# The last inverse stage of a long convolution: 64 outputs per weight, high and low constants side by side

## The chip, the core and the metric

The kernel runs on one core of a Trainium2 chip. Its time is the device time of one execution in microseconds (us), the median of the runs shown. The engines of the core have short names here, as in the profile: PE is TensorE (matmuls; PEld is its loading of weights), ACT is ScalarE, DVE is VectorE, POOL is GpSimd, SP is SyncE. SP does no arithmetic; it issues transfers (DMA). ACT and POOL can issue transfers too, each on a queue of its own. Matmuls write to PSUM, which has eight banks; everything else lives in SBUF, 128 partitions (rows) wide, or in DRAM.

## The reference

Four layers are applied to `x` of 2048 positions by 576 channels. Layers 1 and 3 add a Fourier mixing of the normalised input, layers 2 and 4 add a gated long convolution:

```python
def _A_ref(x, dft_seq_re, dft_seq_im, dft_hid_re, dft_hid_im):
    a = jnp.einsum("bsd,ed->bse", x, dft_hid_re)
    b = jnp.einsum("bsd,ed->bse", x, dft_hid_im)
    return jnp.einsum("ts,bse->bte", dft_seq_re, a) - jnp.einsum("ts,bse->bte", dft_seq_im, b)

def _B_ref(q, k, v, shift_k, ssm_k, ssm_D):
    ...                                    # k_shift: causal convolution of k with 4 taps
    kv = k_shift * v
    y = irfft(rfft(kv, 2 * S) * rfft(ssm_k.T, 2 * S))[:S]    # per channel
    return q * (y + kv * ssm_D)

x = x + _A_ref(_layernorm(x), ...)
x = x + _B_ref(_layernorm(x), B_k, B_v, B_shift_k, B_ssm_k, B_ssm_D)
x = x + _A_ref(_layernorm(x), ...)
x = x + _B_ref(_layernorm(x), B_k, B_v, B_shift_k, B_ssm_k, B_ssm_D)
```

(The transform is written in one line here; the reference uses real FFTs over a padded axis.) What multiplies `q`, the row `y + kv * ssm_D`, does not depend on `x`. Both gated layers use the same one, so the kernel computes it once.

## The kernel before

All data are fp32. A matmul takes its operands rounded to a shorter format (fp32r), so the kernel splits a number into a high part (an ACT copy that rounds) and a low part (a DVE subtraction), and forms high x high, high x low and low x high. The helper `split` does this (L98, L99); `act_split` does it in the stages described here (its lines in the profile are L512 and L518).

**The main line of work** is the first mixing layer (`layer`, L300). A step n of its loop loads one 128x512 block of the sequence matrix (`load_c`, on SP's queue), splits it (L98, L99), and multiplies four column blocks of the input (accumulated in the banks `s0` to `s3`) and a remainder (bank `rm`) with it. A block border comes every 16 steps: the `s` banks are evacuated by ACT and DVE. What results is multiplied by the hidden matrix in halves of 288 columns (`hidden`, L276), 27 matmuls into one bank `bk`, which DVE adds to the residual row (L287).

**The side line** is the long convolution (`branch`, a generator). Whoever runs the main line takes a piece of it whenever its planned share is due: the numbers that the generator yields are planned costs, `I2_COST` = 2.0 for a piece of the last stage. They set the order in which work is laid out, not a time. The convolution is a transform of 4096 points in two steps each way:

- a first stage (`f1_products`) that stores its result `td` in DRAM;
- 64 rounds of a middle stage, 32 for each half of the channels. A round loads a row group of `td` ("feed"), splits it, transforms the kernel's part (`mid_kernel`) and the signal's part (`mid_signal`), multiplies them as complex numbers on DVE (L531 to L534), rounds the product (`mid_round`), transforms it back (`mid_inverse`) and stores it in DRAM as `vd` (L549, ACT's queue). Each transform is three matmuls of 128x288 into one bank `bk`;
- the last inverse stage, 32 products (`i2_products`, L551), one for each half of the channels and each of 16 residues j. A product loads a feed from `vd`, splits it, multiplies it by constants, copies the bank to a tile `vo` and stores that as a piece of the row `yb[j]`.

In the last stage a feed holds two halves c (288 columns each) for 128 frequency rows. The output of a product is 128 positions, so the constants of c are a 128x128 weight `fc[:, c]` (high) and another `fc[:, 2 + c]` (low):

```python
for c in range(2):
    mm(ps[:, :HD], fc[:, c, :], vf[0][:, cs], c == 0, False)
    mm(ps[:, :HD], fc[:, c, :], vf[1][:, cs], False, False)
    mm(ps[:, :HD], fc[:, 2 + c, :], vf[0][:, cs], False, c == 1)
```

**Order and resources.** `feeds` is the list of rounds and products in order: from the 37th round on, every second round is followed by a product of the first half of the channels, ten in all, and the other 22 products stand behind the last round. Constants come on POOL's queue (`load_fr`), feeds on SP's (`load_after`, which places a load behind the latest load of the sequence matrix). The banks `bk` are three and are given out in turn to the hidden halves, the transforms of the middle stage and the products. The ring `vo` has three tiles, shared by `mid_inverse` and the products; a tile is free again when its store has landed. ACT's work on this line is kept in written order (`act`, L509). After the last round, the rings of feeds and constants grow to four tiles each.

Rows of `yb` are read back later, when the gated layers are formed (`gated`, L656).

Of the kernel before, what the change touches and what calls it, by code (L numbers as in the profile page):

```python
# [10 lines left out]
F32 = mybir.dt.float32  # L11
# [4 lines left out]
P = 128  # L16
HP = P // 2
S = 2048
# [47 lines left out]
def fnet_h3_kernel(ctx: ExitStack, tc: tile.TileContext, x, c_mat, w_re, w_im, k_pad, v, shift_k,  # L66
# [16 lines left out]
    def bank():  # L83
        return psp.tile([P, NT], F32, tag="b", bufs=3, name="bk")
# [114 lines left out]
        return t  # L199

    t_d = dr.tile([P, 2 * J, 2 * D], F32, name="td")
    v_d = [dr.tile([P, J, 2, HD], F32, name=f"vd{h}") for h in range(2)]
    yb_d = [dr.tile([P, D], F32, name=f"yb{j}") for j in range(J)]
    xa_d = [dr.tile([P, D], F32, name=f"xa{j}") for j in range(J)]
    xb_d = [dr.tile([P, D], F32, name=f"xb{j}") for j in range(J)]
# [143 lines left out]
    def branch():  # L349
# [142 lines left out]
        at = lay(m1, at, ("yf", D, 2))  # L492
        fc_at = at
        at = lay(flts, SC_AT + CRAW * NT, ("res", D, 2))
        lay(flts, at, ("land", D, 2), ("kk", D, 2), ("vo", HD, 3), ("p2", HD, 1))
        mc = quads(ring["mc"]())
        load_fr(mc, midc)
        lo, hi = slice(0, 64), slice(64, 128)
# [21 lines left out]
        def mid_kernel(df):  # L520
            pk, kk = mid_half(df, HD), two(ring["kk"]())
            act(kk[:, 0, :], pk[:, :HD], AF.Copy)
            act(kk[lo, 1, :], kk[hi, 0, :], AF.Copy)
            act(kk[hi, 1, :], kk[hi, 0, :], AF.Copy, scale=-1.0)
            act(kk[hi, 0, :], kk[lo, 0, :], AF.Copy)
            return kk

        def mid_signal(df, kk):
            px = mid_half(df, 0)
            p1, p2 = kk[:, 0, :], ring["p2"]()  # L530
            nc.vector.tensor_tensor(p1, px[:, :HD], p1, OP.mult)  # L531
            nc.vector.tensor_tensor(p2[lo], px[hi, :HD], kk[hi, 1, :], OP.mult)  # L532
            nc.vector.tensor_tensor(p2[hi], px[lo, :HD], kk[lo, 1, :], OP.mult)  # L533
            nc.vector.tensor_tensor(p1, p1, p2, OP.add)  # L534
            return p1

# [5 lines left out]
        def mid_inverse(hf, qg, yf):  # L542
            pv = bank()
            mm(pv[:, :HD], mc[:, 2, :], yf[:, 0, :], True, False)
            mm(pv[:, :HD], mc[:, 2, :], yf[:, 1, :], False, False)
            mm(pv[:, :HD], mc[:, 3, :], yf[:, 0, :], False, True)
            vo = ring["vo"]()
            act(vo, pv[:, :HD], AF.Copy)
            nc.scalar.dma_start(v_d[hf][4 * qg:4 * qg + 4].rearrange("q j c d -> (q j c) d"), vo)  # L549

        def i2_products(hf, j, fc, vf):  # L551
            yo = ring["vo"]()
            ps = bank()
            for c in range(2):
                cs = slice(c * HD, (c + 1) * HD)
                mm(ps[:, :HD], fc[:, c, :], vf[0][:, cs], c == 0, False)
                mm(ps[:, :HD], fc[:, c, :], vf[1][:, cs], False, False)
                mm(ps[:, :HD], fc[:, 2 + c, :], vf[0][:, cs], False, c == 1)
            act(yo, ps[:, :HD], AF.Copy)
            nc.scalar.dma_start(yb_d[j][:, hf * HD:(hf + 1) * HD], yo)  # L560

        mids = [(0, hf, qg) for hf in range(2) for qg in range(32)]
        late = [(1, 0, j) for j in range(J)]
# [10 lines left out]
        def load_feed(i):  # L574
            if i < len(feeds):
                kind, hf, q = feeds[i]
                landed[i] = ring["land"]()
                load_after(landed[i], v_d[hf][:, q].rearrange("p c d -> p (c d)") if kind else
                           t_d[4 * q:4 * q + 4, :, hf * D:(hf + 1) * D].rearrange("m j d -> (m j) d"))

        def load_fc(k):
            if k < len(rows):
                fcs[k] = quads(ring["fc"]())
                load_fr(fcs[k], i2c[rows[k]])

        def split_feed(i):
# [13 lines left out]
        for i, (kind, hf, q) in enumerate(feeds):  # L600
            df = halves.pop(i)
            if kind:
                i2_products(hf, q, fcs.pop(used), df)
                load_fc(used + ahead)
                used += 1
            else:
                if len(yfs) == MID_LAG:
                    mid_inverse(*yfs.pop(0))
                    yield 0.4
                kk = mid_kernel(df)  # L610
                if product is not None:
                    yfs.append((*product[:2], mid_round(product[2])))
                yield 1.6
                product = hf, q, mid_signal(df, kk)
            split_feed(i + 2)
            if i >= I2_FIRST - 8 and feed_ahead == 3:
                tiles = [ring["land"]() for _ in range(3)]
                if tiles[0] is third:
                    ring["land"], feed_ahead = Ring(tiles[1:]), 2
                    lay(m1, fc_at, ("fc", 4 * P, 2))  # L620
                    load_fc(0)
                    load_fc(1)
            if feed_ahead == 2:
                feed_ahead = 2.5
            else:
                load_feed(i + int(feed_ahead) + 2)
            if i == last_mid:
                yield 0.4
                mid_inverse(*yfs.pop(0))
                yfs.append((*product[:2], mid_round(product[2])))  # L630
                while yfs:
                    yield 0.4
                    mid_inverse(*yfs.pop(0))
                for name, t, at, words in (("fc", m1, spare, 4 * P), ("land", flts, kk_at, D)):
                    old = ring[name]
# [452 lines left out]
def _constants():  # L1088
# [5 lines left out]
    n = (16 * p[None, :, None] + j[:, None, None]) * (4 * q[None, None, :] + 1) % 8192  # L1094
    at = (2 * np.pi * n / 8192).transpose(0, 2, 1)
    at = at[:, np.concatenate([[2 * g, 2 * g + 1, HP + 2 * g, HP + 2 * g + 1] for g in range(HP // 2)])]
# [5 lines left out]
    i1 = np.zeros((2, 2, 2 * J, 2, 2, J, 2))  # L1102
# [6 lines left out]
    th = 2 * np.pi * (j[:, None] * j[None, :] % J) / J  # L1109
    c, s = np.cos(th), np.sin(th)  # L1110
    for a in range(2):
        for b in range(2):
            i1[0, a, b::2, b, a, :, 0] = c
            i1[1, a, b::2, b, a, :, 0] = -s
            i1[0, a, b::2, b, a, :, 1] = s
            i1[1, a, b::2, b, a, :, 1] = c
    m = [*_parts(f2.reshape(P, P)), *_parts(i1.reshape(P, P))]
    return f1c, i2c, np.stack(m, axis=1)

# [39 lines left out]
```

## Time and profile before

| | |
|---|---|
| median of three runs | 1194.99 us (1194.62 to 1196.27) |
| the profiled execution | 1195.03 us, span of its instructions 1193.3 us |
| PE busy | 1172.4 us, 98% of the span |
| DVE busy | 840.3 us, 70% |
| ACT busy | 661.1 us, 55% |
| moved by DMA | 259.85 MB, 218 GB/s over the span |

The page counts an engine as busy while an instruction of it is in flight. Matmuls overlap, so the busy share of PE does not say how fast it works; the chain of waits gives what each matmul costs when they follow one another. In the profile, an instruction is named by its line and by its tiles, output first: `bk<-mid` are the matmuls of the middle and of the last stage (their operands lie in the region `mid`), `bk<-w,u` those of the hidden halves, `s<-mats` and `rm<-mats` those of the main line. `flts` is the region in which `vo`, the feeds and the raw blocks of the sequence matrix lie. L75 is the helper of all matmuls, L168 that of most loads on SP.

### The profile page before, as it was taken

How to read it: one execution, taken by the hardware profiler on the slowest of the kernel's cores; microseconds unless marked ns; L12 is line 12 of the kernel's file. 1: busy time of each engine (PE TensorE's matmuls, PEld its weight loads, DVE VectorE, ACT ScalarE, POOL GpSimd, SP SyncE). 2: the span in 40 equal slices, each digit the busy share in tenths (PEclk: the TensorE clock that was granted, in tenths of full speed). 3: DMA queues.
4: the chain of work that ended last, by engine and by line, in shares of the span. 5: the costliest groups of instructions: out<-in, count | busy, mean ns of one | idle time of the engine just before them, and what ended most of it. 6: DMA issues, size and time to landing. Idle time of an engine off the chain costs nothing.

```text
span 1193.3 us, 18055 instructions
## 1 busy us (share of the span) xinstructions
PE 1172.4 (98%) x6248; PEld 996.3 (83%) x6248; DVE 840.3 (70%) x1498; ACT 661.1 (55%) x1311; POOL 75.6 (6%) x116
## 2 busy tenths in 40 slices
PE   7999999999999999999999999999999999999997
PEld 5776667888888888888988898888888888889997
DVE  7899983679777677685347756865776777774764
ACT  7865655679877668775435666634444445450210
POOL 2210000000000000001101121000000000001111
PEclk9999999999999999999999999999999999999999
DMA  9869898546666656648957676872672777895621
GB/s 327 306 199 311 263 295 269 167 133 188 217 194 211 206 174 203 207 133 272 295 193 236 230 246 226 267 260 71 220 277 76 220 278 258 248 334 158 217 86 41
DMA packets 142846, 259.85 MB, mean 218 GB/s; under 512 B 15649, under 2 KB 43553, under 8 KB 142754
## 3 DMA queue, kind: packets, MB, share of 16 engines
q1 hardware_dynamic: 102674, 205.45, 53.1%
q10 hardware_dynamic: 33168, 42.63, 10.3%
q0 software_dynamic: 6912, 10.62, 3.5%
q8 instruction: 49, 0.80, 0.3%
q14 instruction: 43, 0.35, 0.1%
HBM read 191.99 MB, written 66.65 MB: 217 GB/s over the span
## 4 chain that ended last, share of the span: by engine, by line
PE 76%; ACT 3%; DVE 1%; issue 1%; DMA 0%; POOLq 0%; ACTq 0%; DVEq 0%; SPq 0%
PE s L75 43%; PE bk L75 30%; PE rm L75 4%; ACT flts L512 1%; ACT mid L512 1%; ACT u L98 0%; DMA wd<-w 0%; ACT mats L98 0%; DVE mid L518 0%; DVE flts L534 0%; DVE flts L533 0%; DVE flts L531 0%; DVE flts L532 0%; DVE mats L99 0%; POOLq L1155 0%
## 5 line engine op out<-in xcount | busy, mean ns | idle before, releaser
L75 PE MATMUL s<-mats 128*128 128x512 f32 x2088 | 540.9, 395 | 2.4 <-DVE mats L99 0.8
L75 PEld LDWEIGHTS s<-mats 128*128 128x128 f32 x2088 | 380.9, 188 | 84.8 <-issue 10.4
L99 DVE TENSOR_TENSOR mats<-flts,mats 128x512 fp32r<-128x512 f32 x206 | 141.1, 689 | 63.8 <-ACT mats L98 62.5
L98 ACT ACTIVATE mats<-flts 128x512 fp32r<-128x512 f32 x206 | 128.5, 629 | 82.0 <-PE bk L75 35.0
L75 PE MATMUL bk<-mid 128*128 128x288 f32 x768 | 131.9, 298 | 2.4 <-ACT flts L512 1.6
L75 PEld LDWEIGHTS bk<-mid 128*128 128x128 f32 x768 | 116.9, 188 | 20.0 <-ACT flts L512 6.3
L75 PE MATMUL bk<-w,u 128*128 128x288 f32 x864 | 121.0, 296 | 0.4 <-DVE w L241 0.4
L75 PEld LDWEIGHTS bk<-w,u 128*128 128x128 f32 x864 | 117.5, 188 | 4.0 <-ACT flts L512 1.2
L518 DVE TENSOR_TENSOR mid<-flts,mid 128x576 fp32r<-128x576 f32 (+1 forms) x149 | 93.5, 628 | 34.9 <-ACT mid L512 30.9
L512 ACT ACTIVATE flts<-bk 128x288 f32<-128x288 f32 x160 | 62.1, 404 | 86.8 <-PE bk L75 77.7
L75 PE MATMUL rm<-mats 128*128 128x512 f32 x304 | 94.8, 391 | 0.0
L512 ACT ACTIVATE flts<-flts 64x288 f32<-64x288 f32 x192 | 85.0, 443 | 5.5
L512 ACT ACTIVATE mid<-flts 128x576 fp32r<-128x576 f32 (+1 forms) x148 | 80.4, 575 | 7.6 <-DMA flts<-td 3.2
L451 ACT ACTIVATE flts<-bf 128x384 f32<-128x384 f32 (+1 forms) x104 | 43.2, 463 | 45.6 <-PE bf L75 45.5
L287 DVE TENSOR_TENSOR flts<-flts,bk 128x288 f32<-128x288 f32 x48 | 21.8, 454 | 65.9 <-PE bk L75 65.8
L75 PE MATMUL bk<-mats 128*128 128x288 f32 (+1 forms) x376 | 67.8, 317 | 0.0
L75 PEld LDWEIGHTS rm<-mats 128*128 128x128 f32 x304 | 56.9, 188 | 12.3 <-DVE flts L273 0.2
L75 PE MATMUL s<-t,mats 128*128 128x512 f32 x264 | 64.9, 389 | 0.0
L184 POOL TENSOR_TENSOR flts<-flts 128x1 f32<-128x1 f32 x35 | 29.2, 834 | 522.0 <-DVE flts L183 520.0
L75 PE MATMUL bk<-mats,t 128*128 128x288 f32 (+1 forms) x368 | 59.3, 303 | 0.0
L75 PEld LDWEIGHTS bk<-mats 128*128 128x128 f32 x376 | 55.5, 188 | 3.4
L75 PEld LDWEIGHTS s<-t,mats 128*128 128x128 f32 x264 | 49.5, 188 | 10.3
(145 smaller groups left out, 1467.5 us busy)
## 6 DMA issues: line engine op xcount, KB each, us to landing
flts<-in_c_mat SPq DMA_DIRECT2D x148, 256.0 KB, 3.6
ph<-in_c_mat SPq DMA_DIRECT2D x54, 512.0 KB, 4.5
flts<-in_c_mat SPq DMA_DIRECT2D x30, 512.0 KB, 5.0
flts<-td SPq DMA_DIRECT2D x53, 288.0 KB, 3.0
td<-flts ACTq DMA_DIRECT2D x36, 384.0 KB, 4.5
vd<-flts ACTq DMA_DIRECT2D x64, 144.0 KB, 2.5
flts<-vd SPq DMA_DIRECT2D x32, 288.0 KB, 4.6
mid<-in_i2c POOLq DMA_DIRECT2D x32, 256.0 KB, 4.9
```

The lines of the kernel that those rows point to most:

```text
L75: return nc.tensor.matmul(ps, lhsT, rhs, start=first, stop=last, skip_group_check=more).ins
L98: a = nc.scalar.activation(h, src, AF.Copy).ins
L99: return a, nc.vector.tensor_tensor(l, src, h.bitcast(F32), OP.subtract).ins
L184: pows.append(nc.gpsimd.tensor_tensor(rs, ve, mhalf, OP.pow).ins)
L287: added[:] = [nc.vector.tensor_tensor(r[:, cs], r[:, cs], ps[:, :HD], OP.add).ins]
L451: stored[:] = [nc.scalar.activation(so[:, i, :], ps[i], AF.Copy).ins]
L512: last_act.append(nc.scalar.activation(*args, **kw).ins)
L518: nc.vector.tensor_tensor(l, src, h.bitcast(F32), OP.subtract)
```

## The change

The 128 outputs of a product are divided into two sets of 64: positions 32 n + j and 32 n + 16 + j, with n from 0 to 63. The inverse transform is regrouped to 64 frequencies x 32 residues, so that a set of 64 outputs needs one contraction over 128 rows (real and imaginary part of 64 frequencies) instead of two. One weight of 128 columns then holds the 64 high constants of a set and its 64 low constants, side by side; for the second set the low ones come first.

- A product is four matmuls instead of six: for each set, that weight times the high and times the low part of the feed. Half the rows of the bank then hold the sum with the high constants, the other half the sum with the low ones.
- Each set has a bank of its own. ACT copies the high half of the bank, 64 rows, to `vo`; DVE adds the low half of the bank, which lies in the other 64 partitions. Then these 64 rows are stored, on SP's queue, to every second row of `yb[j]`. There are two stores for a product where there was one on ACT's queue.
- `vd` is laid out by 32 residues. A feed of the last stage is two pieces of 288 numbers per row that lie apart in DRAM instead of one of 576.
- A constant tile has 2 x 128 columns instead of 4 x 128.
- In the middle stage the two copies of the imaginary part exchange their signs, and the second product is written over its input. The tile `p2` is gone; its place is a fourth `vo` tile.

```diff
-    v_d = [dr.tile([P, J, 2, HD], F32, name=f"vd{h}") for h in range(2)]
+    v_d = [dr.tile([P, 2 * J, HD], F32, name=f"vd{h}") for h in range(2)]
...
-        lay(flts, at, ("land", D, 2), ("kk", D, 2), ("vo", HD, 3), ("p2", HD, 1))
+        lay(flts, at, ("land", D, 2), ("kk", D, 2), ("vo", HD, 4))
...
-            act(kk[lo, 1, :], kk[hi, 0, :], AF.Copy)
-            act(kk[hi, 1, :], kk[hi, 0, :], AF.Copy, scale=-1.0)
+            act(kk[lo, 1, :], kk[hi, 0, :], AF.Copy, scale=-1.0)
+            act(kk[hi, 1, :], kk[hi, 0, :], AF.Copy)
...
-            p1, p2 = kk[:, 0, :], ring["p2"]()
+            p1, p2 = kk[:, 0, :], kk[:, 1, :]
             nc.vector.tensor_tensor(p1, px[:, :HD], p1, OP.mult)
-            nc.vector.tensor_tensor(p2[lo], px[hi, :HD], kk[hi, 1, :], OP.mult)
-            nc.vector.tensor_tensor(p2[hi], px[lo, :HD], kk[lo, 1, :], OP.mult)
+            nc.vector.tensor_tensor(p2[lo], px[hi, :HD], p2[lo], OP.mult)
+            nc.vector.tensor_tensor(p2[hi], px[lo, :HD], p2[hi], OP.mult)
...
-            nc.scalar.dma_start(v_d[hf][4 * qg:4 * qg + 4].rearrange("q j c d -> (q j c) d"), vo)
+            nc.scalar.dma_start(v_d[hf][4 * qg:4 * qg + 4].rearrange("m j d -> (m j) d"), vo)
...
-            ps = bank()
-            for c in range(2):
-                cs = slice(c * HD, (c + 1) * HD)
-                mm(ps[:, :HD], fc[:, c, :], vf[0][:, cs], c == 0, False)
-                mm(ps[:, :HD], fc[:, c, :], vf[1][:, cs], False, False)
-                mm(ps[:, :HD], fc[:, 2 + c, :], vf[0][:, cs], False, c == 1)
-            act(yo, ps[:, :HD], AF.Copy)
-            nc.scalar.dma_start(yb_d[j][:, hf * HD:(hf + 1) * HD], yo)
+            ps = [bank() for _ in range(2)]
+            for i in range(2):
+                cs = slice(i * HD, (i + 1) * HD)
+                mm(ps[i][:, :HD], fc[:, i, :], vf[0][:, cs], True, False)
+                mm(ps[i][:, :HD], fc[:, i, :], vf[1][:, cs], False, True)
+            for i, (main, corr) in enumerate(((lo, hi), (hi, lo))):
+                act(yo[main], ps[i][main, :HD], AF.Copy)
+                nc.vector.tensor_tensor(yo[main], ps[i][corr, :HD], yo[main], OP.add)
+                nc.sync.dma_start(yb_d[j][i::2, hf * HD:(hf + 1) * HD], yo[main])
...
-                load_after(landed[i], v_d[hf][:, q].rearrange("p c d -> p (c d)") if kind else
+                load_after(two(landed[i]) if kind else landed[i], v_d[hf][:, q::J, :] if kind else
                            t_d[4 * q:4 * q + 4, :, hf * D:(hf + 1) * D].rearrange("m j d -> (m j) d"))
...
-                fcs[k] = quads(ring["fc"]())
+                fcs[k] = two(ring["fc"]())
...
-                    lay(m1, fc_at, ("fc", 4 * P, 2))
+                    lay(m1, fc_at, ("fc", 2 * P, 2))
...
-                for name, t, at, words in (("fc", m1, spare, 4 * P), ("land", flts, kk_at, D)):
+                for name, t, at, words in (("fc", m1, spare, 2 * P), ("land", flts, kk_at, D)):
...
-    i2 = [_parts(np.cos(at) / S), _parts(-np.sin(at) / S)]
-    i2c = np.stack([i2[0][0], i2[1][0], i2[0][1], i2[1][1]], axis=2)
+    n = np.arange(HP)[None, :] * 32 + np.arange(2 * J)[:, None]
+    at = 2 * np.pi * (n[:, None, :] * (4 * q[None, :HP, None] + 1) % 8192) / 8192
+    i2 = _parts(np.stack([np.cos(at) / S, -np.sin(at) / S], axis=2).reshape(2 * J, P, HP))
+    i2c = np.stack([np.concatenate([i2[0][:J], i2[1][:J]], axis=2),
+                    np.concatenate([i2[1][J:], i2[0][J:]], axis=2)], axis=2)
```

The constants of the inverse transform in the middle stage (`i1`) are regrouped in the same way; its matmuls keep their number and shape.

More of the change, by code (lines that the diff above doesn't have):

```diff
@@ L1093, in _constants @@
     f1c = np.stack(f1, axis=2)
-    n = (16 * p[None, :, None] + j[:, None, None]) * (4 * q[None, None, :] + 1) % 8192
-    at = (2 * np.pi * n / 8192).transpose(0, 2, 1)
-    at = at[:, np.concatenate([[2 * g, 2 * g + 1, HP + 2 * g, HP + 2 * g + 1] for g in range(HP // 2)])]
-    i2 = [_parts(np.cos(at) / S), _parts(-np.sin(at) / S)]
-    i2c = np.stack([i2[0][0], i2[1][0], i2[0][1], i2[1][1]], axis=2)
+    n = np.arange(HP)[None, :] * 32 + np.arange(2 * J)[:, None]
[3 more added lines that the diff above has]
+                    np.concatenate([i2[1][J:], i2[0][J:]], axis=2)], axis=2)
     w = np.arange(2 * J)
@@ L1101, in _constants @@
     f2 = np.zeros((2, 2, 2 * J, 2, 2, 2 * J))
-    i1 = np.zeros((2, 2, 2 * J, 2, 2, J, 2))
+    i1 = np.zeros((2, 2, 2 * J, 2, 2, 2 * J))
     c, s = np.cos(th), np.sin(th)
@@ L1108, in _constants @@
         f2[a, 1, :, 1, a, :] = c
[L1109 to L1116, printed above, removed]
+        i1[0, a, :, a, 0, :] = c
+        i1[1, a, :, a, 0, :] = -s
+        i1[0, a, :, a, 1, :] = s
+        i1[1, a, :, a, 1, :] = c
     m = [*_parts(f2.reshape(P, P)), *_parts(i1.reshape(P, P))]
```

## The prediction

> **What bounds the kernel now.** I read the page first (busy shares, granted clock, chain), then cut out the stretch in which the edited stage runs, then its chain, its groups, its waits and its transfers.
>
> ```profile
> span 1193.3 us, 18055 instructions
> ...
> PE 1172.4 (98%) x6248; PEld 996.3 (83%) x6248; DVE 840.3 (70%) x1498; ACT 661.1 (55%) x1311; POOL 75.6 (6%) x116
> ...
> PEclk9999999999999999999999999999999999999999
> ...
> PE 76%; ACT 3%; DVE 1%; issue 1%; DMA 0%; POOLq 0%; ACTq 0%; DVEq 0%; SPq 0%
> ```
>
> TensorE (PE) is busy for 98% of the span, its granted clock is full throughout, and 76% of the chain that ended last lies on PE. The profiled execution took 1195.03 us, 1.73 us more than its span, and the three runs shown have their median at 1194.99 us: the sum below is made against 1195.
>
> ```profile
> L560 ACTq DMA_DIRECT2D yb<-flts x32: 326/326/830, 390.7 to 609.4; - x32
> ...
> L168 SPq DMA_DIRECT2D flts<-yb x10: 319/352/430, 613.3 to 1109.7; - x10
> ...
> DMA to landing us min/median/max: 1.8/4.1/7.8
> ```
>
> By the transfers of `yb`, the stage stores its outputs between 390.7 and 609.4 us, and the first row is read back at 613.3 us. So I take 388 to 612 us, in two parts: until 548 us ten products (a product is one call of `i2_products`) run between the rounds of the middle stage, and after that the other 22 run without it.
>
> ```profile
> core 0: us, PE busy (x) PEld busy (x) DVE busy (x) ACT busy (x) POOL busy (x), PEclk, DMA share, GB/s
> 388.00:548.00 160.00, 158.97 (x882) 138.16 (x881) 115.95 (x223) 116.62 (x252) 5.80 (x11) 1.00 0.62 187
> 548.00:612.00 64.00, 64.00 (x394) 58.44 (x394) 23.32 (x34) 25.58 (x52) 10.03 (x19) 1.00 0.85 271
> ```
>
> PE is full in both parts. ScalarE (ACT) and VectorE (DVE) are each busy for about 73% of the first part, and for 40% and 36% of the second. The chain of waits through the second part shows what a product costs while PE is the limit:
>
> ```profile
> 560.35 5.20 PE bk L75 x39
> ...
> 587.56 5.20 PE bk L75 x39
> ...
> 596.81 0.79 PE bk L75 x6
> 597.60 2.08 PE s L75 x9
> ...
> 601.63 5.14 PE bk L75 x39
> ```
>
> Six matmuls of a product fill 0.79 us, 0.132 us each, and nine of 128x512 fill 2.08 us, 0.231 us each. A run of 39 is 27 matmuls of the half of a hidden projection and then two products with nothing between them; there are four such runs, from the one at 560.35 to the one at 601.63.
>
> ```profile
> L75 PE MATMUL s<-mats 128*128 128x512 f32 x468 | 124.5, 393 | 0.6 <-DVE u L99 0.5
> ...
> L75 PE MATMUL bk<-mid 128*128 128x288 f32 x459 | 77.9, 298 | 0.6 <-ACT flts L512 0.6
> ...
> L75 PE MATMUL bk<-w,u 128*128 128x288 f32 x312 | 43.7, 295 | 0.0
> ...
> L512 ACT ACTIVATE flts<-flts 64x288 f32<-64x288 f32 x87 | 38.5, 443 | 2.6
> L512 ACT ACTIVATE flts<-bk 128x288 f32<-128x288 f32 x92 | 36.0, 405 | 63.3 <-PE bk L75 59.1 <-DMA yb<-flts 1.6 <-ACT flts L512 1.4
> ...
> L75 PE MATMUL rm<-mats 128*128 128x512 f32 x78 | 24.3, 391 | 0.0
> ...
> L532 DVE TENSOR_TENSOR flts<-bk,flts 64x288 f32<-64x288 f32 x29 | 13.3, 460 | 0.8
> ...
> L533 DVE TENSOR_TENSOR flts<-bk,flts 64x288 f32<-64x288 f32 x29 | 13.1, 451 | 0.4
> L287 DVE TENSOR_TENSOR flts<-flts,bk 128x288 f32<-128x288 f32 x12 | 5.5, 454 | 22.5 <-PE bk L75 22.5
> ```
>
> The mean of one matmul in these rows (298 or 393 ns) is no price, since matmuls overlap; the chain's slots are. With them, 546 matmuls of 128x512 (468 + 78) make 126 us and 771 of 128x288 (459 + 312) make 102 us, together 228 of the 232 us of this window. So at most some 4 us of it is PE waiting or unrecorded: what is taken off PE here comes off the end, and hardly anything else can.
>
> **The change, part by part.**
>
> *Matmuls.* A product goes from six matmuls (two halves c, each high x high, high x low, low x high) to four: two groups of 64 outputs, each with one weight that holds the high and the low constants side by side, times the high and the low input. The moving width stays 288 and the weight stays 128x128, so the price stays 0.132 us. 32 products x 2 x 0.132 = 8.4 us less on PE. This is the only term that lies on the path by itself.
>
> *Evacuation.* Before, a product filled one PSUM bank and left through one ACT copy of 128x288 (405 ns). Now it fills two of the three `bk` banks, and each bank leaves through an ACT copy of 64 rows and then a DVE addition that reads the other 64 rows. The copy of 64 rows from a bank has no row; the nearest are 405 ns (128x288 from a bank) and 443 ns (64x288 out of SBUF), and I take 405, because it has the same source. The DVE addition is like L532 and L533, bank and SBUF into 64 rows: 455 ns. So per product ACT gets 0.41 us more and DVE 0.91 us. Over ten products in the first part that is 4 us on ACT and 9 us on DVE, which goes from 116 to about 125 us of 160; over 22 in the second, 9 and 20 us, DVE from 23 to 43 of 64. Neither becomes full. What counts is how long a bank is held, and for that I take one of the four runs of 39:
>
> ```profile
> 584.82 0.33 SPq L168 DMA_DIRECT2D flts<-in_c_mat  x1
> ...
> 591.00 1.76 PE L75 MATMUL bk<-mid 128*128 128x288 f32 x12
> 591.20 0.45 DVE L287 TENSOR_TENSOR flts<-flts,bk 128x288 f32<-128x288 f32 x1 [2.47 <-PE bk L75]
> ...
> 592.00 0.41 ACT L512 ACTIVATE flts<-bk 128x288 f32<-128x288 f32 x1 [3.99 <-PE bk L75]
> ...
> 596.62 0.63 ACT L98 ACTIVATE mats<-flts 128x512 fp32r<-128x512 f32 x1 [0.84 <-PE rm L75]
> ...
> 597.28 0.69 DVE L99 TENSOR_TENSOR mats<-flts,mats 128x512 fp32r<-128x512 f32 x1 [0.71 <-ACT mats L98]
> ```
>
> Let t = 0 be 591.00, where the slots of the hidden half end. The half's bank is released by L287, 0.20 to 0.65. Today's first product ends its slots at 0.79 and ACT starts on it at 592.00, 0.21 later. DVE follows ACT by 0.03 us (L98 ends 597.25, L99 starts 597.28). After the change: product A fills its banks by 0.26 and 0.53. ACT copies the first from 0.47 to 0.87, DVE adds from 0.90 to 1.36, and at about 1.40 that bank is free. Product B's first bank is the one of the hidden half, free at about 0.69, and its second is A's first. So B starts at 0.69 rather than 0.53, and its second group at 1.40 rather than 0.95; both products end at 1.66 where four matmuls each without waits would end at 1.06. That is 0.60 us lost, in four runs: 2.4 us. In between, products lie 2 us or more apart, with `s` matmuls there (2.08 us ahead of the one at 599.68), and 1.40 us of holding is covered.
>
> In the first part a product stands beside one step of the middle stage instead. For half of the ten products I charge the 0.15 us by which a bank asked for at 0.53 is late: 0.75 us. From below this is nothing (a product among `s` matmuls); from above it is 0.60 us for each of the eight hidden halves there, 4.8 us.
>
> *Middle stage.* The signs of two ACT copies are exchanged, and the second product is formed in place instead of in a tile of its own: the same number of instructions of the same shape, priced at nothing. The freed 288 words become a fourth `vo` tile.
>
> *Stores, loads and queues.* The store of a product moves from the ACT queue to SP and becomes two of 72 KB.
>
> ```profile
> SPq L168 <- DVE mid L518: 103.4, 52, 5.4
> SPq L168 <- DVE mats L99: 41.6, 33, 8.7
> ```
>
> ```profile
> ACT mid L512 <- DMA flts<-td: 3.2, 5, 1.2
> ...
> ACT mid L512 <- DMA flts<-vd: 1.7, 2, 1.0
> ACT flts L512 <- DMA yb<-flts: 1.6, 1, 1.6
> ```
>
> ```profile
> q1 hardware_dynamic: 15123, 30.03, 42.8%
> ...
> q10 hardware_dynamic: 8928, 9.15, 12.3%
> ...
> flts<-in_c_mat SPq DMA_DIRECT2D x39, 256.0 KB, 3.7
> flts<-vd SPq DMA_DIRECT2D x31, 288.0 KB, 4.7
> ...
> yb<-flts ACTq DMA_DIRECT2D x32, 144.0 KB, 3.9
> ```
>
> SP gets 64 issues of about 0.33 us (the row at 584.82), 21 us in 224; it waits for buffers most of the time already, 103 us of it for L518, so issue time is to be had. A store waits for its DVE addition, and behind it in the queue stand the feed loads and the loads of `c_mat`. A feed load is released by an L518 that DVE runs after the same additions, so the store adds two issues, 0.7 us, and hardly a wait. A `c_mat` load issued at 584.82 is first read by the L98 at 596.62: 11.8 us, against 3.7 us to land. That is the cover; it would be gone if a store stood in front for more than 7 us. Feeds have less: ACT waited for `td` and `vd` loads 3.2 and 1.7 us. From above, both waits doubled would be 5 us on ACT, with PE feeding on other matmuls meanwhile; I take nothing. A product's row that reaches DRAM later is read back from 613.3 us on only.
>
> Constant loads halve from 256 to 128 KB, 4 MB less in 32 loads, on POOL's queue; no wait for one stands in the waits of the stretch: nothing. The `vd` load keeps its 288 KB in twice as many pieces. Time per packet follows the bytes here (q1: 42.8% of 16 engines x 224 us over 15123 packets is 101 ns for 1986 B; q10: 49 ns for 1025 B), so I leave it at 4.7 us. The writes of `vd` keep one contiguous block. The one wait for a `yb` store (1.6 us on ACT) should go with the fourth tile; PE did not show it, so it counts as nothing, at best 1.6.
>
> *Sum.* -8.4 + 2.4 + 0.75 = -5.3 us, and 1195.0 - 5.3 = 1189.7 us.
>
> **The rivals.**
>
> *The second bank eats the gain.* Not only the four double products wait but each of the twelve hidden halves costs 0.60 us: 7.2 us; together with half a microsecond at each of the two block borders of the stretch, where ACT and DVE evacuate the `s` banks, that is 8.2 us and the time is 1194.8. For it: DVE is in order, and an addition that stands behind an L99 or L518 that waits for ACT comes later than I reckon. Against it: in the second part DVE is free for 64% of the time. The page "TensorEngine Tiling (Array Packing)", section PSUM Bottleneck, of the Trainium skill states this as a rule: packing speeds up TensorE but not the emptying of PSUM, which may become the bottleneck. By the rows above evacuation per product grows from 0.41 to 1.7 us of engine time while PE shrinks from 0.79 to 0.53, so the trace agrees with its direction; the bank count decides the size.
>
> *The stores hold back ACT.* This is the one that ends slower. A `vo` tile is held for 1.4 us of evacuation, the wait at SP (103.4 us in 52 times, 2.0 us), and a landing of 4.1 us: 7.5 us. Four products of the second part take 4 x 64 / 22 = 11.6 us, so there are 4 us to spare. With the longest wait at SP (5.4 us) and the longest landing (7.8 us) it is 14.6 us, and ACT, in order, waits 3 us at its next copy; then the banks stay full and PE stops. It decides from the point where the 18 products behind the first four lose more than 7.7 us in all (the gain and the bank waits of the sum), 0.43 us each. At half of the 1.6 us that one such wait took today, 0.8 us, it is 14.4 us: 1204. For it: DMA is at 85% in this part, and SP is often parked. Against it: there are four tiles instead of three, and the constants' traffic is halved. The Trainium skill, page "SBUF — State Buffer", section "Can I just issue two DMAs to hit both halves?", speaks for it: a transfer from 64 partitions reaches half of the ports, and two halves run one after the other. By that rule two halves take about twice one whole store, and this rival becomes likelier; the rows of before show no pair of half stores to test it with.
>
> *The gain comes whole.* No bank wait beyond today's: 1195.0 - 8.4 = 1186.6 us, if the order of the matmuls is laid out so that others run while a bank is emptied.
>
> **How the numbers follow.** A measurement of this kernel can tell some 0.2%, 2.4 us, from no change. I give the forecast (1187.5 to 1192.5) 0.58, the whole gain (below 1187.5) 0.10, the gain eaten (1192.6 to 1197.4) 0.13, and the stores that hold back ACT (above 1197.4) 0.19. Faster: 0.68, same 0.13, slower 0.19. From below the range takes in the whole gain and the 1.6 us wait, 1185; from above it cuts into the slower case at 1199, so that about 0.15 is left out above and 0.03 below. The likeliest case alone spans 1187.5 to 1192.5.
>
> **What would show it.** Right: 128 matmuls `bk<-mid` of this stage in place of 192, a chain that still runs over PE from 548 to 612 us, and this part ended some 5 us sooner; new waits of PE for a DVE addition of about half a microsecond, only behind the hidden halves. Wrong: ACT or DVE in the chain between 548 and 612 us, ACT waiting for `yb` stores, or `c_mat` loads that an L98 waits for. If the additions take much more than 455 ns, or stand behind other work of DVE, the first rival holds; if SP's waits grow into ACT's, the second.

## The result and the profile after

| | before | after |
|---|---|---|
| median, nine runs each | 1195.72 us (1193.66 to 1197.07) | 1192.38 us (1190.47 to 1193.42) |
| ratio, 95% interval | | 0.9973 [0.9962, 0.9983] |
| the profiled execution | 1195.03 us, span 1193.3 us | 1192.95 us, span 1190.9 us |

The kernel became 3.3 us (0.27%) faster; 5.3 us were forecast. Runs of one kernel spread by about 3 us here, so most of what follows turns on differences of one to three microseconds, and some of it stays inside the noise.

The page after, its span and busy time:

```profile
span 1190.9 us, 18118 instructions
...
PE 1168.4 (98%) x6184; PEld 986.3 (83%) x6184; DVE 868.3 (73%) x1562; ACT 676.7 (57%) x1343; POOL 75.5 (6%) x116
```

PE has 64 matmuls less (6184 for 6248) and is still busy for 98% of the span. DVE gained 64 instructions and 28 us, ACT 32 and 16 us; 29 and 13 us were counted. In the two parts of the stretch (the columns are those shown of before):

```profile
core 0: us, PE busy (x) PEld busy (x) DVE busy (x) ACT busy (x) POOL busy (x), PEclk, DMA share, GB/s
388.00:548.00 160.00, 157.52 (x859) 134.46 (x858) 124.18 (x241) 119.89 (x260) 6.33 (x12) 1.00 0.61 178
548.00:612.00 64.00, 63.74 (x370) 55.25 (x369) 43.52 (x79) 37.44 (x74) 9.50 (x18) 1.00 0.85 242
```

DVE is busy for 124 of 160 us and 44 of 64, against forecasts of 125 and 43. The two kinds of instruction that empty the banks, in the groups of 380 to 612 us:

```profile
L560 DVE TENSOR_TENSOR flts<-bk,flts 64x288 f32<-64x288 f32 x64 | 29.1, 455 | 3.6 <-ACT flts L512 1.3 <-DMA flts<-vd 0.3
...
L512 ACT ACTIVATE flts<-bk 64x288 f32<-64x288 f32 x64 | 25.9, 404 | 20.7 <-PE bk L75 19.5
```

Both prices are those that were taken from other rows, 455 ns and 405 ns. In the chain of waits the product costs what it should, four matmuls in 0.53 us (568.57 and 571.14):

```profile
551.45 0.69 ACT mid L512
...
552.19 0.40 PE bk L75
...
568.57 0.53 PE bk L75 x4
569.09 2.05 PE s L75 x9
571.14 0.53 PE bk L75 x4
...
585.62 4.17 DMA flts<-vd
589.79 0.68 ACT mid L512
```

But the chain, which before lay on PE from 540 to 615 us throughout, now leaves it, as in the first and the last two of these lines: through ACT's copies and splits and, for 4.17 us, through the landing of a feed. ACT in this chain is a sign that the prediction had named for being wrong. What PE waits for, as the waits of 380 to 612 us have it (total, times, longest), first before and then after:

```profile
PEld bk L75 <- ACT flts L512: 3.6, 9, 0.6
...
PEld bk L75 <- DVE mid L518: 0.5, 2, 0.3
```

```profile
PEld bk L75 <- ACT flts L512: 7.0, 15, 1.2
...
PEld bk L75 <- DVE flts L560: 1.6, 7, 0.4
PEld bk L75 <- DVE mid L518: 1.6, 5, 0.4
```

Waits for ACT's copies, which free banks, nearly doubled, and waits for the additions (L560) came in. To have one number for each trace, I took the time from each matmul's start to the next one's and subtracted its slot (0.132 us for 288 columns, 0.226 us for 512; the medians of both traces are 0.132 and 0.227). What is left over is PE's waiting:

| PE waiting, us | 388 to 548 | 548 to 612 |
|---|---|---|
| before | 5.6 | 0.7 |
| after | 8.9 | 3.3 |

For the whole span I give only the difference, because its 216 matmuls of 384 columns, the same in both kernels, have no slot here: after waits 6.0 us more. So 64 x 0.132 = 8.4 us of matmuls went, 6.0 us of waiting came, and 2.4 us are left: the difference of the two spans. Of the added waiting, 3.3 us came in the first part and 2.6 in the second; 1.2 us lie between 850 and 1100 us (2.4 for 1.2), in the second mixing layer, which the change does not touch; the profiled executions of the experiments have from 0.8 to 4.6 us there. The remaining parts sum to 1 us less than before. So a difference of about 1 us between two single traces can come from neither kernel.

### The profile page after: what moved, and what is told of

Its sections match the earlier page's. It is cut to its first block, busy times and chain, and to the rows that moved or that the text cites. A ratio compares the mean times of both kernels' runs of the same rounds, so it can differ in the third digit from the quotient of the medians.

```text
span 1190.9 us, 18118 instructions
## 1 busy us (share of the span) xinstructions
PE 1168.4 (98%) x6184; PEld 986.3 (83%) x6184; DVE 868.3 (73%) x1562; ACT 676.7 (57%) x1343; POOL 75.5 (6%) x116
## 4 chain that ended last, share of the span: by engine, by line
PE 84%; DVE 5%; ACT 4%; DMA 4%; issue 1%; SPq 0%; POOLq 0%; POOL 0%; ACTq 0%; DVEq 0%
PE s L75 48%; PE bk L75 30%; PE rm L75 5%; PE bf L75 2%; ACT flts L512 2%; DVE f1f L393 1%; DMA flts<-in_c_mat 1%; DVE f1f L398 1%; ACT mid L512 1%; DVE mats L99 1%; DMA t<-ud 1%; DMA flts<-in_w_im 1%; DMA early<-in_x 0%; ACT mats L98 0%; DMA td<-flts 0%
## 5 line engine op out<-in xcount | busy, mean ns | idle before, releaser
L98 ACT ACTIVATE mats<-flts 128x512 fp32r<-128x512 f32 x206 | 128.3, 628 | 83.3 <-PE bk L75 33.0
L75 PE MATMUL bk<-mid 128*128 128x288 f32 x704 | 128.2, 302 | 3.1 <-ACT flts L512 2.5
L75 PEld LDWEIGHTS bk<-mid 128*128 128x128 f32 x704 | 108.3, 188 | 26.0 <-ACT flts L512 8.8
L512 ACT ACTIVATE flts<-bk 128x288 f32<-128x288 f32 (+1 forms) x192 | 75.4, 405 | 74.9 <-PE bk L75 66.6
L518 DVE TENSOR_TENSOR mid<-flts,mid 128x576 fp32r<-128x576 f32 (+1 forms) x149 | 93.6, 629 | 14.0 <-ACT mid L512 11.1
```

The costliest lines, as they stand in the source:

```text
L75: return nc.tensor.matmul(ps, lhsT, rhs, start=first, stop=last, skip_group_check=more).ins
L98: a = nc.scalar.activation(h, src, AF.Copy).ins
L512: last_act.append(nc.scalar.activation(*args, **kw).ins)
L518: nc.vector.tensor_tensor(l, src, h.bitcast(F32), OP.subtract)
```

## The experiments

The theory at this point was that of the banks: two of three banks per product, each held through an ACT copy and then a DVE addition. Its rivals were a cover (the matmuls of the first part only filled time in which PE waits anyway) and SP's queue (slower issues and held-up loads). All ratios are to the kernel before, run on the same chip in the same series. In the table "waiting" is PE's waiting from 388 to 612 us in the one profiled execution, found as above.

| run | median, us | ratio to before, 95% interval | waiting, us |
|---|---|---|---|
| before | 1194.8 to 1195.7 | 1 | 6.3 |
| after | 1192.38 | 0.9973 [0.9962, 0.9983] | 12.2 |
| e1: before with four matmuls | 1188.99 | 0.9947 [0.9934, 0.9959] | 8.0 |
| e2: after without the addition | 1189.48 | 0.9951 [0.9938, 0.9963] | 8.9 |
| e3: after, stores on ACT's queue | 1195.63 | 1.0001 [0.9992, 1.0010] | 13.5 |
| e4: after with six matmuls | 1199.51 | 1.0036 [1.0024, 1.0049] | 11.4 |
| e5: after, products in two pieces | 1191.53 | 0.9967 [0.9955, 0.9980] | 11.1 |
| e6: before, second product in place | 1194.58 | 0.9997 [0.9989, 1.0006] | 6.2 |
| e7: after, whole feeds | 1192.39 | 0.9976 [0.9965, 0.9987] | 11.3 |
| e8: after, one store | 1192.16 | 0.9973 [0.9964, 0.9982] | 11.8 |
| e9: after, all products late | 1190.92 | 0.9966 [0.9952, 0.9979] | 9.3 |
| e10: after, feeds split ahead | 1193.21 | 0.9979 [0.9970, 0.9988] | 10.8 |
| e11: e5 and e10 | 1193.26 | 0.9982 [0.9973, 0.9990] | 9.8 |
| e12: e5 and e9 | 1191.71 | 0.9969 [0.9958, 0.9981] | 9.6 |

**e1, the 64 matmuls alone.**

```diff
                 mm(ps[:, :HD], fc[:, c, :], vf[0][:, cs], c == 0, False)
-                mm(ps[:, :HD], fc[:, c, :], vf[1][:, cs], False, False)
-                mm(ps[:, :HD], fc[:, 2 + c, :], vf[0][:, cs], False, c == 1)
+                mm(ps[:, :HD], fc[:, c, :], vf[1][:, cs], False, c == 1)
```

> The kernel before, with the two matmuls of a product that take the low constants left out: four matmuls, one bank, one ACT copy, one store, so the low half of the constants is missing from the output. It prices the 64 matmuls alone. Theory of the banks (the two banks, each held by ACT and then DVE, take away what the matmuls give): all 8.4 us come off, 1187.3 us against 1195.7, and PE's time between 388 and 612 us holds no more waiting than before. Rival of the cover (in the first part the matmuls of a product only fill time in which PE waits for the middle stage anyway): the ten products of the first part give nothing, at most 5.8 us come off, 1189.9 us or more.

It came to 6.1 us less than the 1195.1 us of before in its series, between 4.9 and 7.9 by the interval; its profiled execution took 1187.5 us, 7.6 us less. The median lies between the two ends, and the interval reaches both, so the time does not decide between them. By the trace, most of the 8.4 us came off, and some 1.5 us turned into waiting in the first part (7.1 us there, 5.6 before). In its waits of 380 to 612 us, PE stands longer for ACT's copies than before although nothing was added:

```profile
PEld bk L75 <- ACT flts L512: 5.2, 10, 1.4
...
PE bk L75 <- ACT flts L512: 1.6, 4, 1.0
```

Most of this is a single stand, in the timeline of e1:

```profile
459.68 0.68 ACT L512 ACTIVATE mid<-flts 128x576 fp32r<-128x576 f32 x1 [2.64 <-DMA flts<-vd]
...
460.71 0.43 PEld L75 LDWEIGHTS bk<-mid 128*128 128x128 f32 x3 [1.38 <-ACT flts L512]
```

ACT had waited 2.64 us for a feed that landed late (the longest such wait of before is 1.0 us), and the copy behind it came late too. From one matmul's start to the next, PE lost 1.1 us there. So some 0.4 us is left for the cover in this trace.

**e4, the change without its saving.**

```diff
                 mm(ps[i][:, :HD], fc[:, i, :], vf[0][:, cs], True, False)
+                mm(ps[i][:, :HD], fc[:, i, :], vf[1][:, cs], False, False)
                 mm(ps[i][:, :HD], fc[:, i, :], vf[1][:, cs], False, True)
```

> The kernel after, with one matmul of each set issued twice (the low half of the feed is counted twice in the output): six matmuls in a product again, all else as after. It prices the change without its saving. Theory of the banks: the evacuation is the same, but the longer product gives it 0.26 us more, so some of the 5.8 us of waiting is covered: 1195.7 + 3 to 5 = 1199 to 1201 us. Rival of the cover: the two matmuls fill the waiting fully, and the time is that of before, 1195 to 1197 us.

The change costs 4.4 us (2.9 to 5.9) when the number of matmuls stays, as the theory of the banks had it, and 64 matmuls lie between this kernel and the kernel after: 4.4 + 3.3 = 7.7 us for them, near the 8.4 of the slots. The full cover is out.

**e2, without the addition.**

```diff
                 act(yo[main], ps[i][main, :HD], AF.Copy)
-                nc.vector.tensor_tensor(yo[main], ps[i][corr, :HD], yo[main], OP.add)
                 nc.sync.dma_start(yb_d[j][i::2, hf * HD:(hf + 1) * HD], yo[main])
```

> The kernel after, without the DVE addition of the low half (it is missing from the output): a bank is free after its ACT copy, some 0.9 us after its matmuls instead of 1.4, and DVE loses 29 us of work. Theory of the banks: about half of the 5.8 us of added PE waiting returns, so 1189 to 1190 us against 1192.4. If the whole trouble is that two banks are taken at once, whoever empties them: 1192. Rival of the SP queue (stores and slower load issues hold back the feeds): no change beyond 1 us, since the stores stay where they are.

It took 5.6 us off the time of before, where the kernel after takes 3.3. The two intervals overlap by a hair, so the share of the addition is about 2.5 us with an uncertainty nearly as large; the traces say the same, 8.9 us of waiting against 12.2, less by 2.4 in the first part and by 0.9 in the second. In the second part the additions are gone, and what PE waits for most are feeds whose split is late. First after, then e2:

```profile
PEld bk L75 <- DVE flts L560: 1.3, 6, 0.4
PEld bk L75 <- DVE mid L518: 1.0, 3, 0.4
...
PEld bk L75 <- ACT mid L512: 0.6, 2, 0.3
```

```profile
PEld bk L75 <- ACT mid L512: 1.0, 2, 0.5
...
PEld bk L75 <- ACT flts L512: 0.5, 2, 0.2
...
PEld bk L75 <- DVE mid L518: 0.4, 2, 0.2
```

**e3, stores on ACT's queue.**

```diff
-                nc.sync.dma_start(yb_d[j][i::2, hf * HD:(hf + 1) * HD], yo[main])
+                nc.scalar.dma_start(yb_d[j][i::2, hf * HD:(hf + 1) * HD], yo[main])
```

> The kernel after, with the two stores of a product on ACT's queue, as the one store was before. Rival of the SP queue (a store takes 0.55 us to issue there and waits for DVE, and the feed loads behind it are late): about 2 us faster than the kernel after, 1190.5 us. Theory of the banks: no gain, 1192 us; or slower, if ACT, which now issues two stores behind a DVE addition each, comes later to the next bank: up to 3 us, 1195.

The whole gain goes. The waits of 548 to 612 us show a part of it:

```profile
ACT flts L512 <- DMA yb<-flts: 11.8, 3, 4.6
...
PEld bk L75 <- DVE flts L560: 3.6, 3, 1.8
...
PE bk L75 <- DVE flts L560: 2.5, 3, 1.6
```

ACT stands 11.8 us in three waits that the profile puts down to `yb` stores, and PE then stands for banks whose addition is late. The timeline shows the longest of the three:

```profile
559.91 5.20 ACTq L561 DMA_DIRECT2D yb<-flts  x5
...
560.35 0.45 DVE L560 TENSOR_TENSOR flts<-bk,flts 64x288 f32<-64x288 f32 x1
...
565.15 0.84 ACT L512 ACTIVATE flts<-bk 64x288 f32<-64x288 f32 x2 [4.61 <-DMA yb<-flts]
```

ACT makes its next copy at 565.15, right behind five stores that it issues from 559.91 to 565.11. The last addition ended at 560.80, so the last three of these stores did not wait for DVE: by the trace's semaphore events, two of them waited until an earlier load of `c_mat` had landed (563.08) and an earlier feed (564.58). A store that must wait before its issue, for an addition or for an earlier transfer, holds up ACT's next copy when it stands in ACT's queue. This is the rival that I had placed on SP's queue, and it is real on ACT's. It explains only a part: of the 4.5 us between the profiled executions of e3 and after, 1.3 us are waiting in the stretch and 2.2 us lie in the later mixing layer (4.6 us of waiting there between 850 and 1100 us), which I can't attribute.

**e5, e9 and e12, where the products stand.** e5 makes a product two pieces, each with one set and one bank, that yield half of `I2_COST` each, so that other work can come between them (the rewritten loop of `i2_products` is not shown); e9 puts all products behind the middle stage; e12 does both.

```diff
-                i2_products(hf, q, fcs.pop(used), df)
+                yield from i2_products(hf, q, fcs.pop(used), df)
...
-            yield I2_COST if kind else 1.1
+            yield I2_COST / 2 if kind else 1.1
```

```diff
-I2_LATE = 6
+I2_LATE = 16
```

> The kernel after, with a product laid out as two pieces of half the planned cost, one set and one bank each, so that other work of the main line can come between them; instructions, evacuation and stores are the same. Theory of the banks (two banks are asked for at once while the third is still held): 1 to 3 us faster than the kernel after, 1189.5 to 1191.5 us, and the added waiting of PE in the second part (2.6 us) goes. Rival of the addition (it is DVE's added work and its place behind other work of DVE that costs, wherever the banks are asked for): 1192.4, no change beyond 1 us.

> The kernel after, with all 32 products behind the middle stage (none in the first part). Waiting of PE above before was 3.2 us in the first part and 2.6 us in the second. If the ten products beside the middle stage lose their saving there (the waits of the middle stage are no longer covered, and DVE is at 84% there), the first part now has the waiting of the middle stage alone, and each product behind it keeps 0.264 - 2.6/22 = 0.15 us: about 1 us faster than the kernel after, 1191.5. Rival: the waits of the middle stage stay where they are, now with even less to cover them, and the time is that of the kernel after or up to 2 us more, 1192.4 to 1194.5.

> All 32 products behind the middle stage, each in two pieces: the two variants whose medians lay below the kernel after (1190.9 and 1191.5 against 1192.4). If each removes waiting of its own (1.5 us in the first part, 1 us of the banks asked for in pairs): 1189.5 to 1190.5 us. If the addition on DVE sets the rest, as the variant with the feeds split ahead showed: 1191, no better than either.

By their medians e5 and e9 are 0.9 and 1.5 us below the kernel after (0.7 and 0.8 us by the ratios), which no interval here can tell from nothing, and together they do no better than one. The traces show where waiting falls: e9 has 9.3 us in the stretch for 12.2. That two banks are asked for at once is not seen to cost in the second part: e5 would have taken its 2.6 us away, and its trace has 3.7 us there against 3.3. The time of e5 alone does not decide this.

**e10 and e11, feeds split three products ahead.** Behind the middle stage, where space is free, a fourth tile for split feeds is added.

```diff
...
-            split_feed(i + 2)
+            split_feed(i + split_ahead)
...
                 ahead = feed_ahead = 4
+                old = ring["df"]
+                ring["df"] = Ring([m1[:, spare:spare + 2 * D]] + [old.tiles[(old.n + m) % 3] for m in range(3)])
+                split_ahead = 3
+                split_feed(i + 3)
```

> The kernel after, with a fourth tile for split feeds behind the middle stage (in the place of the tiles that are free by then), so that a feed is split three products ahead instead of two. In the second part PE waits for ACT's and DVE's splits (0.2 to 0.26 us, behind hidden halves), because two evacuations stand in front of a split on both engines. Theory of the late feed: the waiting of the second part falls from 3.3 to below 2 us, 1 to 1.5 us faster than the kernel after, 1191. Theory of the addition: the bank is the later of the two, no change, 1192.4.

> Both: products laid out in two pieces and a fourth tile for split feeds. If the waits behind hidden halves are bank waits and feed waits in turn, the two together free what each alone does not: 1190 us. If the addition's time on DVE is what counts: 1191.5, as the two pieces alone.

Neither is faster than the kernel after. In e10's waits of 548 to 612 us the late feeds are gone altogether, and PE waits for the additions instead, 2.7 us where the three rows of after make 2.9:

```profile
PEld bk L75 <- DVE flts L560: 2.5, 7, 0.5
...
PE bk L75 <- DVE flts L560: 0.2, 1, 0.2
```

Two limits stand behind one another there, the split of the next feed and the emptying of the bank, both on ACT and DVE, and taking one away shows the other.

**e6, e7 and e8, the parts priced at nothing.**

```diff
# e6, in the kernel before
...
-            nc.vector.tensor_tensor(p2[lo], px[hi, :HD], kk[hi, 1, :], OP.mult)
+            nc.vector.tensor_tensor(p2[lo], px[hi, :HD], p2[lo], OP.mult)
...
# e7, in the kernel after
-                load_after(two(landed[i]) if kind else landed[i], v_d[hf][:, q::J, :] if kind else
+                load_after(landed[i], v_d[hf][:, 2 * q:2 * q + 2, :].rearrange("p c d -> p (c d)") if kind else
# e8, in the kernel after, with yb_d[j] as [2, HP, D]
-                nc.sync.dma_start(yb_d[j][i::2, hf * HD:(hf + 1) * HD], yo[main])
+            nc.sync.dma_start(yb_d[j][:, :, hf * HD:(hf + 1) * HD].rearrange("i n d -> (i n) d"), yo)
```

> The kernel before with the part of the change in the middle stage alone: second product in place, signs of two copies exchanged, four tiles of the ring vo instead of three. The prediction priced it at nothing: 1195 us, within 1 us. Rival: the fourth tile and the missing p2 free ACT or DVE from waiting, up to 1.6 us: 1193.5.

> The kernel after, with each feed of the last stage loaded as 128 pieces of 2304 bytes (two neighbouring residues, so the output is another) instead of 256 pieces of 1152. The prediction priced the pieces at nothing: 1192.4, within 1 us, with the issue of such a load back at 0.32 us instead of 0.57. Rival: SP's longer issues delay loads that ACT waits for: 1 to 2 us faster, 1191.

> The kernel after, with one store of 128 rows for each product on SP's queue, when both additions are done; the row yb is kept in the order of the sets in DRAM and put in order when it is read back. It takes 32 issues from SP. If the issues on SP cost (0.55 us each, 64 of them, in front of feed loads): 1 to 2 us faster than the kernel after, 1191. If they are covered: 1192.4, within 1 us. Should two stores of 64 rows run at half the rate, the landing of the one store takes no longer than that of one of the two (3.7 us).

All three are nothing within what can be measured, about 1 us either way. The issue of a feed load goes from 0.57 us to 0.32 when its pieces are whole (times are min/median/max in ns, after and e7):

```profile
L168 SPq DMA_DIRECT2D flts<-vd x32: 524/566/1168, 377.0 to 593.0; - x32
```

```profile
L168 SPq DMA_DIRECT2D flts<-vd x32: 319/322/671, 377.2 to 592.4; - x32
```

and the stores of a product from two of 0.55 us to one of 0.33 (after and e8, line L561 alone):

```profile
L561 SPq DMA_DIRECT2D yb<-flts x64: 445/547/1604, 391.9 to 606.7; - x64
...
DMA to landing us min/median/max: 1.9/3.7/5.1
```

```profile
L561 SPq DMA_DIRECT2D yb<-flts x32: 319/325/1239, 394.3 to 608.0; - x32
...
DMA to landing us min/median/max: 1.7/3.3/4.7
```

SP had the time: shorter issues and fewer stores do not show in the kernel's time. That no landing is ever on the path is not shown; the chain of after has one (585.62).

## Why the prediction held, and where it was off

- **The number.** The kernel gained 3.3 of the 5.3 us forecast, and its 1192.38 us lie 0.1 us inside the likeliest case that I gave (to 1192.5). That the time still fell there is owed to the width of the case, since one of the three terms was off fourfold. By the gain it is nearer to the forecast (5.3 us) than to the rival in which the second bank eats it (0.2 us); by the time it lies about half way (1189.7 and 1194.8), because the kernel before came to 1195.72 us in nine runs and not 1195.0.
- **64 matmuls at 0.132 us: held in the main.** The chain shows 0.53 us for four. With everything else unchanged 64 matmuls are worth 6.1 us (e1) to 7.7 us (e4 against after) by the medians; the 8.4 taken lie just outside e1's interval (4.9 to 7.9). The prediction took every slot removed as time off the end.
- **Evacuation, second part: 2.4 us forecast, 2.6 us of waiting found, in the place told but not in the form told.** Of the 3.3 us of this part, 2.7 lie within 5.5 us behind its five hidden halves, 0.1 to 0.9 us behind each. But I had four double products each stand 0.60 us for one bank that an addition holds, and without the additions (e2) this part still waits 1.7 us more than before. That the sizes agree so well is in part luck. In the trace, matmuls of the main line were laid between the groups of a double product, and the stall is spread over late banks and late feeds. In this timeline of the kernel after (from 588.45 us), the products behind a hidden half have one and then two `s` matmuls between their groups; 590.51 waits for a split, 591.79 for an addition:

```profile
588.45 0.69 PE L75 MATMUL bk<-mid 128*128 128x288 f32 x4
...
588.98 0.40 PE L75 MATMUL s<-mats 128*128 128x512 f32 x1
...
589.21 0.50 PE L75 MATMUL bk<-mid 128*128 128x288 f32 x2
...
589.54 0.62 PE L75 MATMUL s<-mats 128*128 128x512 f32 x2
...
590.01 0.90 PE L75 MATMUL bk<-mid 128*128 128x288 f32 x3
...
590.51 0.19 PEld L75 LDWEIGHTS bk<-mid 128*128 128x128 f32 x1 [0.31 <-ACT mid L512]
...
591.79 0.30 PEld L75 LDWEIGHTS bk<-mid 128*128 128x128 f32 x2 [0.15 <-DVE flts L560]
```

- **Evacuation, first part: 0.75 us forecast, 3.3 us found. This is the term that failed.** I charged half of the ten products "the 0.15 us by which a bank asked for at 0.53 is late", as if ACT and DVE were at the product's disposal. They are not: ACT and DVE do the middle stage's work in order there, and a copy that frees a bank stands behind whatever of it is late. The longest stand of PE in this part of after:

```profile
465.88 0.69 ACT L512 ACTIVATE mid<-flts 128x576 fp32r<-128x576 f32 x1 [0.70 <-DMA flts<-td]
...
466.47 0.61 ACT L98 ACTIVATE mats<-flts 128x512 fp32r<-128x512 f32 x1
466.51 0.94 DVE L560 TENSOR_TENSOR flts<-bk,flts 64x288 f32<-64x288 f32 x2
...
467.11 0.41 ACT L512 ACTIVATE flts<-bk 128x288 f32<-128x288 f32 x1
...
467.57 0.44 PEld L75 LDWEIGHTS bk<-mid 128*128 128x128 f32 x3 [1.24 <-ACT flts L512]
```

ACT waited for a `td` load, split the feed, split a block for the main line, and only then (467.11) made the copy for which, by the profile, the weight load of 467.57 had stood 1.24 us; from one matmul's start to the next PE lost 1.0 us there. The next longest that before does not have, 0.5 us, begins with a load as well:

```profile
445.38 0.64 ACT L98 ACTIVATE mats<-flts 128x512 fp32r<-128x512 f32 x1 [1.78 <-DMA flts<-in_c_mat]
...
446.04 0.84 ACT L512 ACTIVATE flts<-bk 64x288 f32<-64x288 f32 x2
...
447.08 1.65 PE L75 MATMUL bk<-mid 128*128 128x288 f32 x9 [0.30 <-DVE flts L560]
```

In this part the weight loads of PE waited for ACT's copies 3.0 us in eight waits before and 6.4 us in fourteen after. Without the addition (e2) PE waits 0.8 us more here than before, so some 2.4 of the 3.3 us go with the addition in these traces. How much of that is the addition's own time and how much the late loads (the two stands above) is open: e2 has neither of these two waits, but e5 and e8, which make the additions, have none for `c_mat` either. My bound from above was off too: this part has six hidden halves and not eight, so it was 3.6 us.
- **The loads of `c_mat`: a cover that holds in one part only.** I read 11.8 us between issue and use from one load of the second part. From 445 to 515 us, the loads of the kernel before are issued only 3 to 9 us ahead of their L98. In the kernel after, ACT waits for two of them (380 to 612 us), where before has no such row:

```profile
ACT mats L98 <- DMA flts<-in_c_mat: 2.2, 2, 1.8
```

  This is one more sign that I had named for being wrong. No store is shown to cause it: SP issued the load of the 1.78 us wait at 441.80, and its transfer before that was a feed at 439.48.
- **Rivals.** The "TensorEngine Tiling (Array Packing)" page of the Trainium skill, section PSUM Bottleneck, was a good guide to the direction: without the addition the kernel comes within half a microsecond of e1. But its "bottleneck" is not an engine that is full here; DVE is at 68% in the second part.
- **Stores: not seen to hold back anyone on SP's queue, as forecast; on ACT's they did (e3).** ACT's wait for a `yb` store (1.6 us before) is gone. So the move of the stores, which I had priced as a risk, is what keeps the gain by the medians (1192.38 against 1195.63 us); of that benefit the prediction had nothing. The Trainium skill's page "SBUF — State Buffer", section "Can I just issue two DMAs to hit both halves?", has two halves run one after the other. That does not show at this size: where the trace gives both landings of a product (26 of 32), they lie 0.5 us apart, as the issues do, and the pair has landed 4.2 us after its first issue, against 3.3 us for one store of 128 rows (e8), not twice that.
- **The other signs.** The last store of the stage is issued at 606.7 us instead of 609.4, so the stage ended 2.7 us sooner and not some 5. PE's waits for additions in the second part are of at most 0.4 us and lie behind the hidden halves but for one.
- **Priced at nothing and found nothing:** the in-place product and the fourth tile (e6), the feeds in twice as many pieces (e7), the number of stores (e8). The price of a store's issue was off (0.33 us taken, 0.55 found), hidden as argued.

What stays open: how the waiting of the second part divides into banks and feeds, since removing one brought out the other (e10, e11); how much of the first part is late loads; and whether the 0.8 to 1.5 us of e9 are real. No version here is shown to be faster than the kernel after.

## What to carry to other kernels

When PE is the bound, most of the time of matmuls that are taken out comes off the end, but count the instructions that the saving adds to the engines that empty PSUM, and look for the in-order neighbour that stands in front of them, not for a full engine: here a 455 ns addition on an engine that is busy for 68 to 78% of the time took back about 2.5 of 8.4 us, with an uncertainty nearly as large. Price a new wait separately in each stage, by the lateness that this stage already shows in the waits of PE, and read the cover of a load in each stage too. And a store that must wait before its issue belongs on a queue whose engine has no bank to free.

## What was not expected of the hardware

- The issue of a transfer on SP depends on its shape: 0.32 us for a feed of 128 pieces, 0.57 us for the same bytes in 256 pieces (e7 against after), and 0.55 us for 64 rows that go to every second row in DRAM against 0.33 us for 128 rows that go to neighbouring ones (e8).
- With 64 matmuls less and nothing added, PE's waits for ACT's copies rose from 3.6 to 5.2 us (e1). The largest piece, 1.1 us of PE's time, stands behind one feed that landed late.
